# adaLN block with a spectral filter and an MLP, forward and backward: the last phase's operands, layouts and fillers rearranged

## The chip, the cores and the metric

The kernel runs on one core of a Trainium2 chip. The metric is the device time of one execution in microseconds (us). The kernel before took 500.65, 500.38 and 498.91 us in three runs: a median of 500.38. The profile is of one more execution, which took 503.03 us.

## The reference

The program computes a block and its gradients. Both come from this function and its vector-Jacobian product with `grad_out`.

```python
# x: (1, 2048, 512); c: (1, 512); w_mod: (512, 6*512); F = 1792
sa, ca, ga, sb, cb, gb = (silu(c) @ w_mod).reshape(1, 6, 1, 512) along axis 1
h = layernorm(x) * (1 + ca) + sa
x = x + ga * irfft2(rfft2(h) * (w_r + 1j * w_i))       # filter: 2048 x 257
h = layernorm(x) * (1 + cb) + sb
x = x + gb * (relu(h @ w1 + b1)**2 @ w2 + b2)
out_0 = x
out_1 .. out_9 = gradients of x, w_r, w_i, w1, b1, w2, b2, c, w_mod
```

All inputs and outputs are bf16.

## The kernel before

**Tiling.** The 2048 tokens are 16 tiles of 128 rows (NT = 16), in four blocks of 512 (NB = 4). F is 14 chunks of 128 (NFC = 14). The two-dimensional Fourier transform is a chain of matmuls with small DFT matrices. One dimension of 2048 is split as 16 x 128, so the spectrum is worked off in eight groups `gi`, each of which has a filter tile `Z[gi]` of 128 x 2 x 2 x 258 elements.

**Phases.** (1) Start-up: modulation rows, first layernorm, first DFT step (F1). (2) Spectral forward, `spec_f23`: for each group psB (L274) is evacuated to AE (L283, L285), psC (L261) uses AE and the DFT matrix LF, and `cmul` on DVE multiplies by Z. Matmuls of w2T and gT (L621, 224 of them, written to `gab`) serve as a filler here and in the next phase. `spec_g1` (L301, L314) uses a second matrix, LG. (3) `stage_g` and `stage_t` make the rows of the second layernorm from L332 and L346, block by block. (4) The MLP phase: `stage_h` (L771), `stage_o` (L794 with w2) and `stage_gn` (L794 with w1T), four blocks; `f1_again` and `late_f1` do the first DFT step of the backward pass there. (5) The last phase: the spectral backward `spec_f23` with filler `grad_w1` (L966, 256 matmuls) and `grad_b1` (L941, L953), then `spec_g1`, then for each pair of row tiles L332, L346 and the layernorm's backward rows, with filler `grad_w2` (L1037, 224 matmuls), `grad_b2` (L1048), and `GMod` (L413 to L425), which makes one of six column blocks of w_mod's gradient. The row sums acc1 (L1097) go over all 16 tiles, and the first two blocks of GMod need them.

**What sets the order.** Every engine runs its instructions in a fixed order, which is chosen when the program is built from the written order, priorities and a model of durations. All DMAs are issued by SyncE (SP), one after the other: an issue that waits for its data, or for its buffer, holds all DMAs written behind it. Eight DMA semaphores rotate, so a DMA also waits for the eighth DMA ahead of it to land. SBUF pools are stacked on the left and on the right; a tile that takes the place of an older one waits for the older one's last reader. So the place of a pool, too, decides when a load can start.

**The lines the change touches.** `load` (L989 to L992) reads, for one group of the last phase, a slice of LF (`LFb`), the filter in four to six pieces (`load_w`, L493) and the forward spectrum (`Xb`). Two groups are loaded ahead. `h2_sb` (h_sb in the profile, L998) is the operand of `grad_w1`, and `ghn_part` (L761) transposes the other operand, seven DMAs for each block. `load_hn` (L1032) transposes an operand of `grad_w2`, g_sb is the other. `n1` (L1080) and `gxl` are the rows that each pair needs. `w1T` (L666) is the transposed weight for `stage_gn`, w1 (L674) that of `stage_h`, `x1` (L693) the rows of x for `stage_g`.

Of the kernel before, what the change touches and what calls it, by code (L numbers as in the profile page):

```python
# [18 lines left out]
D = 512  # L19
# [142 lines left out]
def build_lf(tc, K, cpool, g):  # L162
# [32 lines left out]
    K["LF"] = LF  # L195
# [53 lines left out]
def spec_f23(tc, K, UT, AEs, dc, dest, elementwise, after=lambda gi: None):  # L249

    nc = tc.nc
    with tc.tile_pool(name="psB", bufs=1, space=PSUM) as psB_pool, \
         tc.tile_pool(name="psC", bufs=2, space=PSUM) as psC_pool:
        def f3(gi):
            ae = AEs[gi % 2]
            tl = dest(gi)
            for hh in range(2):
                ps = psC_pool.tile([P, 2, 512], FP32, name="psC")
                for o in range(2):
                    for cs in range(2):  # L260
                        nc.tensor.matmul(ps[:, o, 0:DF], lhsT=K["LF"][:, 2 * gi + hh, o + cs, :], rhs=ae[:, hh, 256 * cs:256 * cs + DF],  # L261
                                         start=(cs == 0), stop=(cs == 1))
                nc.scalar.copy(out=tl[:, hh, :, 0:DF], in_=ps[:, :, 0:DF])
# [137 lines left out]
class GMod:  # L401
# [3 lines left out]
    def __init__(self, tc, K, scf, gsc, wm_view, out9_view):  # L405
        self.__dict__.update(locals())

    def emit(self, jc, q, row, pool, ppool):
# [8 lines left out]
        for dc in range(0, 4, 2):  # L417
            wmc = pool.tile([P, 2, D], BF16, name="wmc", bufs=4)
            nc.sync.dma_start(wmc, self.wm_view[:, dc:dc + 2, cs])
            gwm = pool.tile([P, 2, D], BF16, name="gwm", bufs=4)  # L420
            for i in range(2):
                nc.scalar.activation(gwm[:, i, :], psb, AF.Copy, scale=self.scf[:, dc + i:dc + i + 1])
# [6 lines left out]
def kernel(  # L429
# [10 lines left out]
    gx1_dram = dram.tile([P, NT, D], BF16, name="gx1_dram")  # L440
    xs_dram = dram.tile([P, 8, 2, 2, FP], BF16, name="xs_dram")
# [71 lines left out]
    for b in range(NB):  # L513
# [94 lines left out]
    nc.sync.dma_start(LF_dram, K["LF"])  # L608
# [56 lines left out]
    w1T = wp.tile([P, NFC, D], BF16, name="w1T")  # L665
    nc.sync.dma_start(w1T, B_w1, transpose=True)  # L666
# [7 lines left out]
    nc.sync.dma_start(w1, w1_view)  # L674
    with tc.tile_pool(name="psR", bufs=1, space=PSUM) as psR, tc.tile_pool(name="psO", bufs=2, space=PSUM) as psO_pool, \
# [13 lines left out]
        def load_rows(b):  # L689
# [4 lines left out]
            if b > 0:  # L694
                gbt[b - 1] = rows.tile([P, TB, D], BF16, name="gb")
# [200 lines left out]
        for b in range(NB):  # L896
# [8 lines left out]
            else:  # L905
# [18 lines left out]
    K["LF"] = lf2.tile([P, 16, 3, P], BF16, name="LFb")  # L924
    lg2 = tc.alloc_tile_pool(name="lg2", bufs=1, side="right")
    K["LG"] = lg2.tile([P, 16, 3, P], BF16, name="LGb")
# [3 lines left out]
    h2_sb = gwa.tile([P, NT, D], BF16, name="h2_sb")  # L930
# [14 lines left out]
    def add_quadrants(ps, pool, out, scale=None):  # L945
# [5 lines left out]
        ps = mmps.tile([P, SB], FP32, name="mm")  # L951
        for i, x in enumerate((b4, b4l)):
            nc.tensor.matmul(ps[0:1, 0:w], lhsT=K["ones_col"], rhs=x, start=(i == 0), stop=(i == 1))  # L953
        row = pool.tile([1, w], BF16, name="b4r", bufs=2)
        nc.scalar.copy(out=row, in_=ps[0:1, 0:w])
        if scale is not None:
            nc.vector.tensor_tensor(row, row, scale, op=ALU.mult)
        nc.sync.dma_start(out, row)
# [16 lines left out]
    for fp in range(0, NFB, 2):  # L975
        for dc in range(4):
            for fb in (fp, fp + 1):
                units.append(lambda fb=fb, dc=dc: (grad_w1(fb, dc), dc == 3 and grad_b1(fb)))

    def fill_w1(n):  # L980
        for _ in range(n):
            if units:
                units.pop(0)()

    with tc.tile_pool(name="f23b", bufs=2) as fr, tc.tile_pool(name="ewb", bufs=2) as ew:
        Xt = {}

        def load(gi):
            nc.sync.dma_start(K["LF"][:, 2 * gi:2 * gi + 2], LF_dram[:, 2 * gi:2 * gi + 2])  # L989
# [8 lines left out]
        nc.sync.dma_start(h2_sb, h2_dram)  # L998
# [176 lines left out]
```

## Time and profile before

| what | value |
|---|---|
| median of three runs | 500.38 us |
| the profiled execution | 503.03 us, its span 501.3 us |
| mean granted TensorE clock | 0.968 |
| MLP phase, by the order of PE's lines | about 134 to 311 us |
| last phase: spectral backward | about 311 to 399 us |
| last phase: row tiles and grad_w2 | about 399 to 501 us |

The span is the time from the first to the last instruction. Times in the rows below are microseconds from its start unless marked ns. PE is TensorE's matmuls, PEld its weight loads, DVE VectorE, ACT ScalarE, SPq the DMA queue of SyncE. In an order row, `out<-in` names the tiles without buffer numbers, and the profile calls several tiles by short names: w is w1 or w2, h_dram may be h2_dram, n is n1, x is x1.

In the windows of 10 us, PE is busy 10.00 for most of 130 to 311, at a granted clock of 1.00. It has more gaps, and a clock under 1.00, in the last phase.

### The profile page before, as it was taken

Reading aid. Unit: us, or ns where it says so; the run is one execution under the profiler, and the core shown is the slowest. Engines: PE = TensorE matmul, PEld = TensorE weight load, DVE = VectorE, ACT = ScalarE, POOL = GpSimd, SP = SyncE. Lnnn points to the kernel's source line nnn. Section 1 sums busy time; section 2 is a strip of 40 time slices with the busy share of each in tenths; the row PEclk is TensorE's granted clock in tenths of the full one; section 3 lists DMA queues with packets and bytes.
Section 4 is the critical chain, followed back from the end, with each engine's and each line's share of the span. In section 5 each row is a group of like instructions: output and inputs, shape, how many; then the busy total and the mean of one; then the engine's idle time right before and its main releaser. Section 6 shows DMA issues by size and latency. Waiting matters only on the chain. (4 is left out here: it accounts for less than half of the span.)

```text
span 501.3 us, 7176 instructions
## 1 busy us (share of the span) xinstructions
PE 444.4 (89%) x2485; PEld 220.8 (44%) x2485; DVE 327.9 (65%) x747; ACT 264.8 (53%) x474; POOL 12.4 (2%) x56
## 2 busy tenths in 40 slices
PE   0848999999999999999979999699699899499993
PEld 0424466545444434434434444355255554144431
DVE  5878899588463577774958484174346464489946
ACT  3456766687461485466537563444242376267342
POOL 4121100000000000000000000000000000000000
PEclk9969999999999999999999999899799899799999
DMA  8964869931199499499349948756665399948995
GB/s 284 237 161 99 306 187 274 345 87 44 62 316 282 105 207 307 124 212 300 104 116 210 303 96 153 259 124 153 166 140 195 113 277 201 268 150 253 252 254 186
DMA packets 151708, 99.11 MB, mean 198 GB/s; under 512 B 99570, under 2 KB 137976, under 8 KB 151032
## 3 DMA queue, kind: packets, MB, share of 16 engines
q1 hardware_dynamic: 151672, 98.66, 73.5%
q8 instruction: 19, 0.31, 0.3%
q14 instruction: 17, 0.14, 0.1%
HBM read 35.43 MB, written 39.61 MB: 150 GB/s over the span
## 5 line engine op out<-in xcount | busy, mean ns | idle before, releaser
L621 PE MATMUL mm<-gT,w2T 128*128 128x512 bf16 x224 | 54.9, 378 | 2.3 <-ACT gab L626 1.1
L966 PE MATMUL mm<-gab,h_sb 128*128 128x448 bf16 x256 | 54.3, 370 | 1.2 <-DMA h_sb<-h_dram 1.2
L771 PE MATMUL mm<-h2T,w 128*128 128x512 bf16 x224 | 52.9, 379 | 2.6 <-DMA h2T<-h_dram 1.9
L1037 PE MATMUL mm<-g_sb,hn 128*128 128x512 bf16 x224 | 51.6, 382 | 1.8 <-DVE gw L1040 1.8
L794 PE MATMUL og<-w,h 128*128 128x512 bf16 x224 | 52.0, 379 | 0.0
L794 PE MATMUL og<-w1T,gab 128*128 128x512 bf16 x224 | 50.3, 379 | 0.0
L772 ACT ACTIVATE r<-mm,b1col 128x512 bf16<-128x512 f32 x56 | 37.9, 685 | 15.1 <-PE mm L771 10.2
L966 PEld LDWEIGHTS <-h_sb 128*128 128x128 bf16 x256 | 25.6, 102 | 26.0 <-issue 4.8
L771 PEld LDWEIGHTS <-w 128*128 128x128 bf16 x224 | 21.1, 97 | 32.2 <-issue 9.2
L1037 PEld LDWEIGHTS <-hn 128*128 128x128 bf16 x224 | 21.0, 98 | 30.2 <-issue 6.7
L794 PEld LDWEIGHTS <-gab 128*128 128x128 bf16 x224 | 21.9, 98 | 25.2 <-DVE gab L778 0.5
L621 PEld LDWEIGHTS <-w2T 128*128 128x128 bf16 x224 | 21.3, 97 | 25.6 <-issue 6.3
L794 PEld LDWEIGHTS <-h 128*128 128x128 bf16 x224 | 21.0, 98 | 24.9 <-issue 2.3
L774 DVE TENSOR_TENSOR h<-r 128x1024 bf16<-128x1024 bf16 x28 | 19.3, 691 | 16.8 <-ACT r L772 16.7
L624 DVE CAST gab<-mm 128x512 bf16<-128x512 f32 x28 | 19.2, 686 | 12.1 <-PE mm L621 11.7
L970 ACT CAST gw<-mm 128x448 bf16<-128x448 f32 x16 | 8.5, 533 | 31.5 <-PE mm L966 31.5
L423 DVE SCALAR_TENSOR_TENSOR gm_junk<-wmc,onef,gmbc 128x512 bf16<-128x512 bf16 x24 | 17.9, 748 | 8.2 <-DMA wmc<-in_w_mod_dram 7.1
L335 ACT ACTIVATE Tsb<-psT 128x512 bf16<-128x512 f32 x32 | 18.4, 599 | 7.9 <-PE psT L332 7.9
L379 DVE TENSOR_TENSOR p<-Z,G 128x1028 bf16<-128x1028 bf16 x8 | 5.6, 699 | 25.9 <-ACT AE L283 13.5
L626 ACT CAST gab<-mm 128x512 bf16<-128x512 f32 x28 | 16.4, 584 | 10.2 <-PE mm L621 10.0
L858 ACT CAST o<-og 128x512 bf16<-128x512 f32 x16 | 9.3, 581 | 20.9 <-PE og L794 20.9
L545 PE MATMUL mod_ps<-wm,scb 128*128 128x512 bf16 x24 | 9.6, 515 | 10.9 <-DVE scb L536 7.7
(265 smaller groups left out, 787.1 us busy)
## 6 DMA issues: line engine op xcount, KB each, us to landing
h_dram<-h SPq DMA_DIRECT2D x28, 256.0 KB, 3.5
gh_dram<-gab SPq DMA_DIRECT2D x28, 256.0 KB, 3.3
w<-in_B_w_dram SPq DMA_DIRECT2D x2, 1792.0 KB
wm<-in_w_mod_dram SPq DMA_DIRECT2D x3, 1024.0 KB, 9.4
wmc<-in_w_mod_dram SPq DMA_DIRECT2D x12, 256.0 KB, 3.8
out_dram<-gwm SPq DMA_DIRECT2D x12, 256.0 KB, 3.9
xs_dram<-Xs SPq DMA_DIRECT2D x8, 258.0 KB, 3.2
Xb<-xs_dram SPq DMA_DIRECT2D x8, 258.0 KB, 4.0
```

The costliest lines, as they stand in the source:

```text
L335: nc.scalar.activation(Tsb, ps, AF.Copy, scale=EF_S)
L423: nc.vector.scalar_tensor_tensor(out=junk, in0=wmc[:, i, :], scalar=K["onef"], in1=gmbc, op0=ALU.mult, op1=ALU.mult, accum_out=self.gsc[:, ...
L545: nc.tensor.matmul(ps, lhsT=scb[:, dc, :], rhs=wmt[j // 2][:, dc, (j % 2) * D:(j % 2 + 1) * D], start=(dc == 0), stop=(dc == 3))
L621: nc.tensor.matmul(ps, lhsT=w2T[:, dc, fc * P:(fc + 1) * P], rhs=gT[b][:, dc, :], start=(dc == 0), stop=(dc == 3))
L624: nc.vector.tensor_copy(out=gaT[b][:, fc, :], in_=ps)
L626: nc.scalar.copy(out=gaT[b][:, fc, :], in_=ps)
L771: nc.tensor.matmul(ps, lhsT=w1[:, dc, (fc + i) * P:(fc + i + 1) * P], rhs=h2T[b][:, dc, :], start=(dc == 0), stop=(dc == 3))
L772: nc.scalar.activation(r[:, i, :], ps, AF.Relu, bias=b1col[:, fc + i:fc + i + 1])
L774: nc.vector.tensor_tensor(h2, r, r, op=ALU.mult)
L794: nc.tensor.matmul(ps, lhsT=lhs(fc), rhs=rhs[:, fc, :], start=(fc == 0 and init is None), stop=(fc == NFC - 1))
L966: nc.tensor.matmul(ps[:, 0:W4], lhsT=h2_sb[:, t, dc * P:(dc + 1) * P], rhs=ghn[t // 4][:, t % 4, fs], start=(t == 0), stop=(t == NT - 1))
L1037: nc.tensor.matmul(ps, lhsT=hns[fc][:, t, :], rhs=g_sb[:, t, :], start=(t == 0), stop=(t == NT - 1))
```

## The change

1. In phase 1 each filter tile Z is also written to `wz_dram`, in the group's own layout (eight DMAs of 258 KB, after POOL has cleared the pad). In the last phase one DMA of 258 KB reads a group's Z.
2. LF for the last phase is in eight tiles. Four are loaded during the end of the MLP phase, four at the start of the last phase.
3. `w1T` moves to a pool of its own, which is released after the last `stage_gn`; its SBUF lies where LF and others were. `gb` moves to the pool of w2. `h2_sb` is loaded behind the last `stage_gn`, and the seven transposes of block 3 are merged into the last `stage_o`.
4. Four groups of Z and Xb are loaded ahead; LG is loaded one group earlier.
5. The second half of `grad_b1` and of `grad_b2` (the ones_col matmuls) is put off by one unit of filler; `grad_b1` is spread over other units.
6. Four of six `GMod` blocks are written into the spectral backward, at odd groups. The scaled rows `gwm` come from the bf16 copy in SBUF, half on ACT and half on DVE.
7. `n1` and `gxl` are loaded two pairs ahead; hn and g_sb are asked for ahead of `spec_g1`; the L332 step of the next pair is written ahead of its filler.
8. acc1 is summed in four quadrants of the array, even and odd rows apart, and the odd half is added at the end.

The core of the diff:

```diff
@@ phase 1
             for gi in range(8):
+                nc.gpsimd.memset(Z[gi][:, :, :, DF:FP], 0.0)
                 load_w(gi)
+                nc.sync.dma_start(wz_dram[:, gi], Z[gi])
@@ MLP phase, pools
-    w1T = wp.tile([P, NFC, D], BF16, name="w1T")
-    nc.sync.dma_start(w1T, B_w1, transpose=True)
...
     hring = tc.alloc_tile_pool(name="hring", bufs=7)
+    w1tp = tc.alloc_tile_pool(name="w1tp", bufs=1)
+    w1T = w1tp.tile([P, NFC, D], BF16, name="w1T")
+    nc.sync.dma_start(w1T, B_w1, transpose=True)
@@ MLP phase, end
+                K["LF"] = [cdp.tile([P, 2, 3, P], BF16, name=f"LFb{gi}") for gi in range(4)]
+                for gi in range(4):
+                    nc.sync.dma_start(K["LF"][gi], LF_dram[:, 2 * gi:2 * gi + 2])
                 merge(stage_gn(b, UT), [x for p in zip(again, parts + [lambda: None]) for x in p])
-                merge(stage_o(b), [lambda: None, lambda: None, late_f1.flush, lambda: None])
+                w1tp.release()
+                h2p = tc.alloc_tile_pool(name="h2p", bufs=1, side="right")
+                h2_sb = h2p.tile([P, NT, D], BF16, name="h2_sb")
+                nc.sync.dma_start(h2_sb, h2_dram)
+                parts = [lambda fc=fc: ghn_part(b, fc) for fc in range(0, NFC, 2)]
+                merge(stage_o(b), [x for p in zip([lambda: None] * 3 + [late_f1.flush] + [lambda: None] * 3, parts) for x in p])
@@ last phase, loads
-            nc.sync.dma_start(K["LF"][:, 2 * gi:2 * gi + 2], LF_dram[:, 2 * gi:2 * gi + 2])
-            load_w(gi)
-            Xt[gi] = fr.tile([P, 2, 2, FP], BF16, name="Xb")
+            if gi >= 4:
+                nc.sync.dma_start(K["LF"][gi], LF_dram[:, 2 * gi:2 * gi + 2])
+            nc.sync.dma_start(Z[gi], wz_dram[:, gi])
+            Xt[gi] = fr.tile([P, 2, 2, FP], BF16, name="Xb", bufs=4)
             nc.sync.dma_start(Xt[gi], xs_dram[:, gi])
-        for gi in range(2):
+        for gi in range(4):
             load(gi)
-        for fc in range(0, NFC, 2):
-            ghn_part(NB - 1, fc)
-        nc.sync.dma_start(h2_sb, h2_dram)
...
-            if gi + 2 < 8:
-                load(gi + 2)
-            if gi == 5:
+            if gi + 4 < 8:
+                load(gi + 4)
+            if gi == 4:
                 nc.sync.dma_start(K["LG"], LG_dram)
-            if gi > 0:
-                fill_w1(2)
+            fill_w1(2 if gi > 0 else 0)
+            if gi % 2 == 1:
+                gms.pop(0)()
@@ GMod
             for i in range(2):
-                nc.scalar.activation(gwm[:, i, :], psb, AF.Copy, scale=self.scf[:, dc + i:dc + i + 1])
+                if i == 0:
+                    nc.scalar.activation(gwm[:, i, :], gmbc, AF.Copy, scale=self.scf[:, dc + i:dc + i + 1])
+                else:
+                    nc.vector.tensor_scalar(gwm[:, i, :], gmbc, self.scf[:, dc + i:dc + i + 1], None, op0=ALU.mult)
@@ last phase, rows
+    load_rows3(0)
     load_hn()
     nc.sync.dma_start(g_sb, g_view)
+    load_rows3(2)
     for _ in range(3):
         load_hn()
+    CS = utcs.tile([P, NT, 4, 16, 8], BF16, name="utcs")
+    spec_g1(tc, K, Z, CS)
...
+        def colsums1(t, gh1, q1):
+            for q, row in ((0, gh1[:, 0, :]), (32, q1[:, 0, :]), (64, gh1[:, 1, :]), (96, q1[:, 1, :])):
+                nc.tensor.matmul(acc1[q:q + 32, :], lhsT=K["ones_q"], rhs=row, start=(t == 0), stop=(t == NT - 2), tile_position=(0, q))
...
+        Ts = g2_pair(0)
+        for t in range(0, NT, 2):
+            fill(1)
+            row_pair(t, Ts)
+            Ts = g2_pair(t + 2)
+            fill(1 if t % 4 == 0 and t < 12 else 0)
+            if t == 10:
+                grad_b2()
+        fill(1)
         late.flush()
-        acc1_sb = fp.tile([P, D], BF16, name="acc1_sb", bufs=1)
-        nc.vector.tensor_copy(acc1_sb[0:64, :], acc1[0:64, :])
+        acc1_odd = fp.tile([64, D], FP32, name="acc1_odd", bufs=1)
+        nc.scalar.copy(out=acc1_odd, in_=acc1[64:128, :])
+        acc1_sb = fp.tile([64, D], BF16, name="acc1_sb", bufs=1)
+        nc.vector.tensor_tensor(acc1_sb, acc1[0:64, :], acc1_odd, op=ALU.add)
```

The change also moves instructions on each engine. Three places follow, with the line numbers of the program they are from.

SP, between the spectral forward and `stage_g`, before: the last writes of the spectrum and of LG, then w1 (w_1473) and the rows of x.

```order
L635 DMA LG_dram<-LG 128x1536
L649 DMA xs_dram<-Xs 128x1032
L674 DMA w_1473<-in_B_w_dram 128x4x1792
L693 DMA x_1485<-in_A_x_dram 128x2048
L693 DMA x_1606<-in_A_x_dram 128x2048
L696 DMA gb<-in_grad_out_dram 128x2048 x2
```

The same place of SP in the changed program:

```order
L643 DMA LG_dram<-LG 128x1536
L657 DMA xs_dram<-Xs 128x1032
L680 DMA_TRANSPOSE w1T<-in_B_w_dram 128x14x512
L657 DMA xs_dram<-Xs 128x1032
L683 DMA w_1493<-in_B_w_dram 128x4x1792
L702 DMA x_1505<-in_A_x_dram 128x2048
L702 DMA x_1626<-in_A_x_dram 128x2048
```

The transpose of w1T, which stood eight rows later behind w2, now stands ahead of the last write of the spectrum, of w1 and of x.

SP, from the MLP phase's end into the last phase, before (gx_dram, rows of the gradient; out_dram<-x, rows of out_0; Z_3384, group 0's filter):

```order
L832 DMA gx_dram<-n2rows 128x1024
L761 DMA_TRANSPOSE gab<-gh_dram 128x4x256 x7
L832 DMA gx_dram<-n2rows 128x1024
L869 DMA out_dram<-x_2460 128x1024
L989 DMA LFb<-LF_dram 128x768 x2
L998 DMA h_sb<-h_dram 128x8192
L869 DMA out_dram<-x_2460 128x1024
L989 DMA LFb<-LF_dram 128x768 x3
L493 DMA Z_3384<-in_A_w_r_dram 64x2x257
```

The same stretch in the changed program:

```order
L922 DMA LFb_3097<-LF_dram 128x768
L889 DMA o<-gx_dram 128x1024 x2
L841 DMA gx_dram<-n2rows 128x1024
L927 DMA h_sb<-h_dram 128x8192
L770 DMA_TRANSPOSE gab<-gh_dram 128x4x256
L841 DMA gx_dram<-n2rows 128x1024
L770 DMA_TRANSPOSE gab<-gh_dram 128x4x256 x4
L878 DMA out_dram<-x_2480 128x1024
L770 DMA_TRANSPOSE gab<-gh_dram 128x4x256 x2
```

h_sb now stands ahead of the seven transposes, and four LFb loads (the last is shown) ahead of the two o loads.

PE, at the row sums of one pair of tiles in the last phase, before (gh and q are the rows that are summed):

```order
L1097 LDWEIGHTS ones_q
L1097 MATMUL acc_4296<-gh_4397,ones_q 32x512
L1097 LDWEIGHTS ones_q
L1097 MATMUL acc_4296<-q_4398,ones_q 32x512
L953 LDWEIGHTS ones_col
L953 MATMUL mm<-b_4483,ones_col 1x448
L1097 LDWEIGHTS ones_q
L1097 MATMUL acc_4296<-gh_4397,ones_q 32x512
L1097 LDWEIGHTS ones_q
L1097 MATMUL acc_4296<-q_4398,ones_q 32x512
```

A pair in the changed program:

```order
L1125 LDWEIGHTS ones_q
L1125 MATMUL acc_4450<-gh_5036,ones_q 32x512
L1125 LDWEIGHTS ones_q
L1125 MATMUL acc_4450<-q_5037,ones_q 32x512
L1125 LDWEIGHTS ones_q
L1125 MATMUL acc_4450<-gh_5036,ones_q 32x512
L1125 LDWEIGHTS ones_q
L1125 MATMUL acc_4450<-q_5037,ones_q 32x512
L1065 LDWEIGHTS hn
```

The four matmuls of a pair, each on a quadrant of its own, now stand together.

More of the change, by code (lines that the diff above doesn't have):

```diff
@@ L194, in build_lf @@
     LF = cpool.tile([P, 16, 3, P], BF16, name="LF")
-    K["LF"] = LF
+    K["LF"] = [LF[:, 2 * gi:2 * gi + 2] for gi in range(8)]
+    K["LFall"] = LF
     for q in range(4):
@@ L923 @@
     lf2 = tc.alloc_tile_pool(name="lf2", bufs=1, side="right")
-    K["LF"] = lf2.tile([P, 16, 3, P], BF16, name="LFb")
-    lg2 = tc.alloc_tile_pool(name="lg2", bufs=1, side="right")
-    K["LG"] = lg2.tile([P, 16, 3, P], BF16, name="LGb")
+    K["LF"] += [lf2.tile([P, 2, 3, P], BF16, name=f"LFb{gi}") for gi in range(4, 8)]
     W4 = 448
@@ L1094 @@
             nc.vector.tensor_tensor(q1, gh1, n1, op=ALU.mult)
+            late.add(lambda: colsums1(t, gh1, q1))
             for i in range(2):
-                late.add(lambda t=t + i, a=gh1[:, i, :], b=q1[:, i, :]: [
-                    nc.tensor.matmul(acc1[q:q + 32, :], lhsT=K["ones_q"], rhs=row, start=(t == 0), stop=(t == NT - 1), tile_position=(0, q))
-                    for row, q in ((a, 0), (b, 32))])
                 jk = fp.tile([P, D], BF16, name="jk1", bufs=1)
```

119 lines of the change are left out of this document (69 added, 50 removed).

## The prediction

> **What bounds the kernel now.** The profile page comes first, for the engine that sets the span.
>
> ```profile
> span 501.3 us, 7176 instructions
> PE 444.4 (89%) x2485; PEld 220.8 (44%) x2485; DVE 327.9 (65%) x747; ACT 264.8 (53%) x474; POOL 12.4 (2%) x56
> ```
>
> PE is busy for 89% of the span, and the change keeps all 2485 matmuls. So it can gain in three ways only: less PE idle time, fewer matmuls at a reduced clock, more matmuls side by side. The profiled execution took 503.03 us, 1.73 beyond its span and 2.65 above the median of the three runs (500.38). I sum against 503.03 and take 2.65 off at the end. The next view is what PE waited for from 305 us, where the last phase begins (columns: total, times, longest).
>
> ```profile
> PE acc L1097 <- DVE q L1094: 6.4, 1, 6.4
> PE psC L261 <- DMA LFb<-LF_dram: 4.3, 1, 4.3
> PE psB L274 <- ACT AE L283: 3.5, 3, 1.5
> PE mm L1132 <- DVE gcb L1130: 2.6, 1, 2.6
> PE psG L301 <- DVE utcs L306: 2.4, 1, 2.4
> PE mm L1037 <- DVE gw L1040: 1.8, 1, 1.8
> PE mm L966 <- DMA h_sb<-h_dram: 1.2, 1, 1.2
> PE mm L413 <- ACT gwm L422: 1.0, 2, 0.8
> PE mm L953 <- ACT b L949: 0.4, 1, 0.4
> ```
>
> These nine rows add up to 23.6 us, and each is a place that the change touches. The third view is the table by windows of 10 us (busy time and count of PE, PEld, DVE, ACT, POOL, then the granted clock, DMA share, GB/s).
>
> ```profile
> 320.00:330.00 10.00, 8.80 (x45) 4.71 (x45) 1.77 (x3) 3.78 (x7) 0.00 (x0) 0.83 0.54 165
> 340.00:350.00 10.00, 10.00 (x61) 5.85 (x60) 5.90 (x12) 4.36 (x9) 0.00 (x0) 1.00 0.63 138
> 390.00:400.00 10.00, 7.76 (x69) 5.13 (x69) 5.78 (x12) 3.37 (x6) 0.00 (x0) 0.83 0.32 107
> 430.00:440.00 10.00, 6.07 (x24) 2.06 (x24) 6.82 (x18) 2.25 (x4) 0.00 (x0) 0.66 0.90 283
> ```
>
> After each of the larger waits the granted clock falls, so a wait costs more than its idle time. An undisturbed window (340 to 350) has 1.00. The price shows in single rows of the timeline of PE:
>
> ```profile
> 357.99 4.29 PE L966 MATMUL mm<-gab,h_sb 128*128 128x448 bf16 x11
> 407.50 1.31 PE L966 MATMUL mm<-gab,h_sb 128*128 128x448 bf16 x6
> ```
>
> At full clock six of these take 1.31 with a drain of about 0.35, so 0.19 each; eleven would take 2.3 and took 4.29 after the wait at 356.99.
>
> **The change part by part: gains.**
>
> *Start of the last phase.* The operand h_sb is asked for late, on SP's queue (start, time):
>
> ```profile
> 295.36 10.01 SPq L761 DMA_TRANSPOSE gab<-gh_dram  x7
> 312.19 0.43 SPq L998 DMA_DIRECT2D h_sb<-h_dram  x1
> ```
>
> It is issued at 312.19, behind ten microseconds of transposes, so L966, the filler that could cover the three AE waits, cannot run before 322. The change issues it ahead of the transposes, when the last w1T matmul ends (about 295). Then L966 stands ready at 311 and covers 3.5 + 1.2 = 4.7 of idle time, and the 0.83 clock of 320:330 (0.17 x 10 = 1.7) goes. What is late next is the first evacuation in the phase, about 0.9 that nothing hides. Gain 5.5; the bounds are 2 (the AE waits stay) and 6.4.
>
> *LF and Z.* The 4.3 wait for LFb has its cause in these rows of SP's own waits:
>
> ```profile
> SPq L1006 <- DVE gW L382: 8.0, 2, 5.1
> SPq L493 <- DMA out_dram<-x: 6.3, 1, 6.3
> SPq L989 <- PE og L794: 4.0, 1, 4.0
> ```
>
> SP issues in order; an L1006 output that waits for DVE holds the LFb and Z loads behind it. With four groups in hand, and one Z load in place of four to six, a load has three to four groups (8 us of PE each) to spare. Gain 4.3 of waiting and 2.6 of clock (2.0 on the eleven matmuls above, 0.6 on their neighbours): 6.9. The eight writes and reads of Z cost SP about 0.4 each beside PE work; I count nothing, since SP idles between the loads there, and 0.4 x 8 = 3 if it did not.
>
> *G1.* The 2.4 wait for utcs comes from DVE standing behind gc work that waited for output DMAs. In the new order the gc work stands behind all the utcs evacuations, so it can hold none of them; the DMAs go out as before. I take 2.4 plus 0.17 x 10 = 1.7 of clock, less 0.3: 3.8 (bounds 0 and 4.1).
>
> *n1.* The 6.4 wait is q for an n load issued behind three hn transposes; now n1 is fetched two pairs ahead. Gain 6.4 + 0.4 (the b wait, deferred) + clock: the 430:440 window at 0.66, of which PE worked 6.07, loses about 2.2. Together 9.0.
>
> *End.* The 1.8, the 1.0 and the 2.6 rows: four of six modulation blocks leave the end, so DVE is free for gw, and L1037 fills between the last two. Of 5.4, I leave 1.0 for the gcb chain: 4.4. The blocks themselves move to the spectral phase, where DVE is 5.90 of 10 busy (340:350).
>
> ```profile
> L423 DVE SCALAR_TENSOR_TENSOR gm_junk<-wmc,onef,gmbc 128x512 bf16<-128x512 bf16 x24 | 17.9, 748 | 8.2 <-DMA wmc<-in_w_mod_dram 7.1
> ```
>
> A block has four of these (3.0) and, new on DVE, two scalings of the same shape; each is bounded by nothing and by the 0.75 of this row. That is 3.0 to 4.5 per block, one block in two groups (16 us): DVE goes from 5.9 to about 8.5 of 10. Hidden, but the cover is thin: each DVE wait that shows costs its length, counted under new waits.
>
> *Row sums.* The matmuls on acc stand like this now, in two quadrants, and, in the MLP phase, four at once:
>
> ```profile
> 438.83 0.39 PE L1097 MATMUL acc<-q,ones_q 128*32 128x512 bf16 x1
> 438.83 0.39 PE L1097 MATMUL acc<-gh,ones_q 128*32 128x512 bf16 x1
> 439.06 0.38 PE L1097 MATMUL acc<-q,ones_q 128*32 128x512 bf16 x1
> 439.37 2.98 PE L1037 MATMUL mm<-g_sb,hn 128*128 128x512 bf16 x13
> 443.15 0.39 PE L1097 MATMUL acc<-gh,ones_q 128*32 128x512 bf16 x1
> ...
> 311.22 0.39 PE L682 MATMUL acc<-gp,ones_q 128*32 128x512 bf16 x1
> ...
> 311.45 0.38 PE L682 MATMUL acc<-gp,ones_q 128*32 128x512 bf16 x1
> ```
>
> Four matmuls of one pair hold PE for 0.23 + 0.31 + 0.38 = 0.92 (the fourth alone, at 443.15). Four at once, as L682, hold it for 0.23, and 0.31 up to a full-array matmul. Eight pairs save 8 x 0.6 = 4.9; one add at the end and an evacuation of acc1's odd half cost about 0.9 that L1037 only partly hides. Gain 3.8 (3 to 5).
>
> Gains: 5.5 + 6.9 + 3.8 + 9.0 + 4.4 + 3.8 = 33.4.
>
> **Costs.**
>
> *Early phase.* w1T is placed where LF was, and its load moves from 135 us to a place ahead of the last xs_dram write, w1 and x:
>
> ```profile
> 79.87 1.06 PE L261 MATMUL psC<-AE,LF 128*128 128x257 bf16 x8
> 87.83 0.37 SPq L649 DMA_DIRECT2D xs_dram<-Xs  x1
> 88.30 0.42 SPq L674 DMA_DIRECT2D w<-in_B_w_dram  x1
> 90.62 0.28 PE L314 MATMUL psF<-LG,Z 128*1 128x128 bf16 x8
> 98.77 0.69 DVE L717 TENSOR_TENSOR yg<-y,modb 128x1024 bf16<-128x1024 bf16 x1 [0.51 <-DMA x<-in_A_x_dram]
> 135.10 11.62 SPq L666 DMA_TRANSPOSE w1T<-in_B_w_dram  x1
> 124.66 9.97 PE L621 MATMUL mm<-gT,w2T 128*128 128x512 bf16 x44 [0.26 <-ACT gab L626]
> ```
>
> w1T may go when the last L261 has read LF, 10.0 us before G1 ends (80.9 to 90.9). Its issue took 11.62 at 135, behind the 1.8 MB of w2; half of that, about 6, is the lower end. So it ends 4.0 before to 1.6 after G1's end. w1 follows at -3.5 to +2.1; now w1 goes out at 2.6 before G1's end, and x is there 10 us after w1 (88.30 to 98.26), when DVE has already waited 0.51. So x comes 0.9 earlier to 4.7 later. The row of xs_dram has the same spread, and ACT's first Tsb waits for that write. Behind the waiting DVE L717 stand the evacuations L624 of the filler, and PE behind them, so a wait passes on nearly whole. From issue near 8.5, between the ends, 1.8 of waiting. Also 57 of the L621 fillers (0.227 each, 12.9 us) move ahead of G1: no more work, but the tail at 124.66, in which DVE and ACT could catch up, goes; 1.2 for that, 1 for the clock. Cost 4.0, bounds -1 and 9.
>
> In sentences that the sum does not need: the Trainium skill, "DMA: Bandwidth & Descriptors", section "Latency and other measured facts", gives a DMA transpose 261 GB/s, by which the 1.8 MB of w1T take an estimated 7.0 us. By that x would wait 0.3 in place of 1.8.
>
> *End of the MLP phase.* Four LFb loads of 0.4 stand ahead of the loads that DVE L881 waits for:
>
> ```profile
> 283.72 3.60 SPq L880 DMA_DIRECT2D o<-gx_dram  x2
> 287.98 0.69 DVE L881 TENSOR_TENSOR o<-o,modb 128x1024 bf16<-128x1024 bf16 x1 [5.30 <-DMA o<-gx_dram]
> ```
>
> 1.6 later, of which PE's order leaves about 0.6 of slack: cost 1.0 (0 to 2).
>
> *New waits in the last phase.* g_sb, hn, n1 and the blocks' loads now come together around G1, so something is late that was not. The nearest rows are the waits that go, so one is bounded by 0 and 6.4. I take one of 2 us and 1 of clock: 3.0.
>
> Costs 8.0; net 25.4. 503.03 - 25.4 = 477.6, less 2.65: **475**.
>
> On the clock: the window 390:400 shows 0.83 after a wait of only 2.4. The Trainium skill, "TensorE: Matmul & The Clock Gate", "HAM oscillation — how this bites in real kernels", has the clock fall for PE gaps over about 3.4 us. By the trace a new wait of 2 us carries clock loss; by the page it carries none, the 2 us of it above go, and the time is 473. The row speaks against the page here.
>
> **The rivals.**
>
> 1. *The early phase costs nothing* (w1T's issue takes 6, x comes in time) and no new wait shows: 475 - 4 - 3 = 468. For it: DVE waits only 0.51 for x now, and lower bounds are met. Against: the row of 11.62.
> 2. *DVE and DMA become the limit* in stage_g and the last phase: early cost 9, new waits of 6.4 with clock 2.2: 475 + 5 + 5.6 = 486. For it: DVE near 8.5 of 10 and the loads crowded at G1. Against: PE has long filler there.
> 3. *The start wait stays* (the change doesn't do what it says): h_sb and seven transposes share the DMA, and the first L966 still waits. Price: the 5.5 of that term: 480.
> 4. *Slower than before.* SP's order holds Z or Xb in every group of the spectral phase: each load stands behind outputs that wait for DVE, as L1006 did for 8.0. Eight waits of 2 are 16; a clock as in 430:440 (0.66) over the phase's 88 us (311 to 399) loses 30: 475 + 46 = 521. It decides once a group's wait is over about 1 us. Against: four groups' lead, some 30 us.
>
> **How the numbers follow.** Forecast 0.60, rivals 0.13, 0.12, 0.10 and 0.05. The forecast with its bounds spans 466 to 484; rival 1 at 468 and 3 at 480 lie in it. The range goes to 464 below (rival 1 with fuller gains) and 488 above (rival 2), so that about 0.15 is left out. 0.5% is 2.5 us, about what a measurement of this kernel can tell from no change. Faster 0.95; of rival 4's 0.05, where only half of the groups wait the time comes out near no change: same 0.02, slower 0.03.
>
> **What would show it.** Right: the waits of L1097, L261 and L301 gone, L966 within 3 us of the last L794, acc in groups of four, granted clock 1.00 from 311 on. Wrong: DVE's L717 waiting over 5 for x or ACT for xs_dram; PE idle ahead of L1037 for g_sb or hn; DVE's p waiting for Z in several groups; PE waiting for L881 over 2.

## The result, and the profile after

The changed kernel took 475.89 us (median of 4 runs, 475.21 to 476.55) against 500.51 for the kernel before in the same comparison: a ratio of 0.9512, with a 95% interval of 0.9483 to 0.9542. Its profiled execution took 475.21 us, 27.8 less than that of before (503.03); the prediction had 477.6 for it and 475 for the median.

First the head of the profile page of the changed kernel, then what PE waited for from 312 us to the end (total, times, longest).

```profile
span 473.4 us, 7172 instructions
PE 432.9 (91%) x2485; PEld 218.3 (46%) x2485; DVE 331.2 (70%) x759; ACT 257.0 (54%) x463; POOL 12.7 (3%) x64
```

```profile
PE psC L262 <- ACT G L264: 3.1, 1, 3.1
PE psB L275 <- ACT AE L284: 0.5, 2, 0.4
PE psG L302 <- ACT utcs L309: 0.2, 1, 0.2
```

The nine rows of before (23.6 us) have become three (3.8 us). One of them is new. The windows say the same of the clock (columns as in the prediction):

```profile
320.00:330.00 10.00, 6.79 (x35) 3.65 (x34) 2.66 (x6) 4.68 (x9) 0.00 (x0) 0.83 0.72 221
430.00:440.00 10.00, 10.00 (x70) 4.94 (x67) 9.47 (x19) 4.59 (x11) 0.00 (x0) 1.00 1.07 279
```

Of the windows from 310 to 470, only the one with the new wait is under 1.00; the window 430 to 440, at 0.66 before, is full. To see where the time went, the program is cut at five places that both kernels have. These are PE's timeline rows of the changed kernel at these places: the last forward psF, the first matmul with w1T, the last with w2, the last backward psF, the last of grad_w2.

```profile
104.43 0.28 PE L315 MATMUL psF<-LG,Z 128*1 128x128 bf16 x8
163.14 12.25 PE L803 MATMUL og<-w1T,gab 128*128 128x512 bf16 x56
311.56 3.20 PE L803 MATMUL og<-w,h 128*128 128x512 bf16 x14
391.99 0.33 PE L315 MATMUL psF<-LGb,Z 128*1 128x128 bf16 x10
462.83 7.08 PE L1065 MATMUL mm<-g_sb,hn 128*128 128x512 bf16 x32
```

And the same places of the kernel before (the first of them stands in the prediction, at 90.62):

```profile
160.20 12.25 PE L794 MATMUL og<-w1T,gab 128*128 128x512 bf16 x56
308.10 3.19 PE L794 MATMUL og<-w,h 128*128 128x512 bf16 x14
398.90 0.28 PE L314 MATMUL psF<-LGb,Z 128*1 128x128 bf16 x8
491.51 3.61 PE L1037 MATMUL mm<-g_sb,hn 128*128 128x512 bf16 x16 [1.84 <-DVE gw L1040]
```

Start plus time, or the start alone for the first w1T matmul, give the cuts and the stretches between them:

| stretch | before | after | difference | predicted |
|---|---|---|---|---|
| start to first w1T matmul ("early") | 160.20 | 163.14 | +2.9 | +4.0 |
| to the last w2 matmul ("MLP") | 151.09 | 151.62 | +0.5 | +1.0 |
| to the last backward psF ("spectral") | 87.89 | 77.56 | -10.3 | -13.2 |
| to the end of grad_w2 ("row part") | 95.94 | 77.59 | -18.4 | -15.6 |
| tail | 6.18 | 3.49 | -2.7 | -1.6 |

In the predicted column, spectral is the sum of the start, LF and Z, and G1 less the new waits, the row part has n1, the row sums and 2.8 of the end, and the tail has the rest of the end. The last psF is the end of G1 in the kernel before, where no psG matmul follows it. In the changed kernel 24 of the 64 psG matmuls still follow:

```profile
392.45 2.78 PE L302 MATMUL psG<-LGb,Z 128*128 128x256 bf16 x24
```

They end at 395.23. With the cut there, the spectral stretch takes 80.5 (7.4 less than before) and the row part 74.7 (21.3 less). Some other work moved from the row part into the spectral stretch: four L413 (L415 in the changed kernel) of about 0.3, and two `grad_b1` of 0.94 with their ones_col matmuls, some 4 us. With all of it counted where it was, the spectral stretch gained about 11.4 (13.2 predicted), and the row part and the tail together about 20.0 (17.2 predicted).

### The profile page after: what moved, and what is told of

Read it like the earlier page. It is cut to its first block, busy times and chain, and to the rows that moved or that the text cites. A ratio compares the mean times of both kernels' runs of the same rounds, so it can differ in the third digit from the quotient of the medians.

```text
span 473.4 us, 7172 instructions
## 1 busy us (share of the span) xinstructions
PE 432.9 (91%) x2485; PEld 218.3 (46%) x2485; DVE 331.2 (70%) x759; ACT 257.0 (54%) x463; POOL 12.7 (3%) x64
## 4 chain that ended last, share of the span: by engine, by line
PE 65%; DVE 11%; DMA 8%; ACT 6%; SPq 5%; issue 2%; POOL 1%; DVEq 0%; ACTq 0%
PE og L803 13%; PE mm L1065 10%; PE mm L780 10%; PE mm L993 10%; PE mm L629 3%; PE psG L302 3%; PE psC L262 2%; PE psT L333 2%; PE psY L347 2%; SPq L770 2%; PE psB L275 2%; DMA o<-gx_dram 2%; DVE l_st L569 2%; DMA n_dram<-x_sb 1%; DMA x<-in_A_x_dram 1%
## 5 line engine op out<-in xcount | busy, mean ns | idle before, releaser
L993 PE MATMUL mm<-gab,h_sb 128*128 128x448 bf16 x256 | 52.8, 360 | 0.0
L1065 PE MATMUL mm<-g_sb,hn 128*128 128x512 bf16 x224 | 50.2, 380 | 0.0
L993 PEld LDWEIGHTS <-h_sb 128*128 128x128 bf16 x256 | 25.4, 99 | 22.0 <-issue 1.8
L816 ACT CAST G<-og 128x512 bf16<-128x512 f32 x16 | 9.3, 580 | 19.0 <-PE og L803 19.0
L347 PE MATMUL psY<-Tsb,TAT 128*128 128x256 bf16 x128 | 18.1, 272 | 1.5 <-ACT Tsb L336 1.4
```

Source lines behind the costliest of these rows:

```text
L347: nc.tensor.matmul(psY[:, H * s:H * s + H], lhsT=K["TAT"][:, s * e], rhs=Tsb[:, H * e:H * e + H], start=(e == 0), stop=(e == 1))
L993: nc.tensor.matmul(ps[:, 0:W4], lhsT=h2_sb[:, t, dc * P:(dc + 1) * P], rhs=ghn[t // 4][:, t % 4, fs], start=(t == 0), stop=(t == NT - 1))
L1065: nc.tensor.matmul(ps, lhsT=hns[fc][:, t, :], rhs=g_sb[:, t, :], start=(t == 0), stop=(t == NT - 1))
```

## The experiments

Every experiment is the changed kernel with one edit, unless it says otherwise. The table gives the stretches of each run's profiled execution, worked out from the same five places, and the median time with that of the kernel before measured beside it. Runs with the same number in the last column were measured on one chip (496.20, 498.08 and 497.04 are of three chips).

| run | forward G1 ends | G1 to first w1T | MLP | spectral | row part | tail | median us | before |
|---|---|---|---|---|---|---|---|---|
| after | 104.7 | 58.4 | 151.6 | 77.6 | 77.6 | 3.5 | 475.89 | 500.51 |
| after_again | 104.2 | 58.4 | 151.7 | 77.5 | 77.6 | 3.5 | 475.39 | 497.04 |
| w1t_behind | 107.2 | 55.1 | 153.7 | 77.1 | 77.4 | 4.1 | 472.78 | 496.20 |
| h2_late | 104.2 | 57.6 | 154.3 | 75.1 | 77.4 | 3.7 | 474.32 | 496.20 |
| h2_place | 107.7 | 58.3 | 151.2 | 78.9 | 77.6 | 3.6 | 478.83 | 497.04 |
| two_ahead | 105.1 | 58.5 | 151.3 | 75.2 | 77.4 | 3.7 | 474.42 | 496.20 |
| z_pieces | 106.7 | 58.2 | 152.0 | 84.7 | 77.4 | 3.7 | 484.36 | 496.20 |
| acc_two | 104.6 | 58.2 | 154.8 | 75.5 | 79.0 | 3.7 | 475.62 | 498.08 |
| no_prefetch | 104.3 | 57.9 | 154.0 | 74.3 | 83.6 | 3.8 | 479.32 | 498.08 |
| gm_end | 107.3 | 58.1 | 151.6 | 78.7 | 74.6 | 20.2 | 490.85 | 498.08 |
| gm_mid | 104.7 | 57.9 | 152.3 | 77.8 | 91.4 | 3.5 | 490.44 | 497.04 |
| g_low | 107.5 | 57.1 | 152.5 | 76.6 | 78.0 | 3.7 | 476.50 | 498.08 |
| best | 106.9 | 55.6 | 151.5 | 73.7 | 77.6 | 3.7 | 469.89 | 497.04 |

The first column and the MLP column vary by over 3 us in code that the edits leave alone, so a median cannot show an effect of one or two. The stretch that an edit touches can, where it is steady in the runs that leave it alone. G1 to the first w1T matmul is (57.1 to 58.5), and so is the row part (77.4 to 78.0). The spectral stretch is not: it takes 74.3 to 77.6 in five runs with the same spectral code (after, after_again, w1t_behind, acc_two, no_prefetch), so it shows no effect under about 3.

The 24 psG matmuls behind the last psF, 2.9 us to their end, stand in the row part of every run but gm_end and gm_mid, where G1 is done at the cut. Beside these two, the changed kernel's stretches are 80.5 and 74.7.

### The early stretch: w1t_behind

```diff
-    nc.sync.dma_start(w1T, B_w1, transpose=True)
...
         load_rows(0)
+        nc.gpsimd.tensor_copy(w1T[:, 0, 0:1], x1b[0][:, 0, 0:1])
+        nc.sync.dma_start(w1T, B_w1, transpose=True)
         merge(stage_g(0))
```

> The changed kernel, but the transposed load of w1T is held back until the first rows of x are in (a one-element copy of x1 on POOL writes into w1T first). Changed kernel: 475.9 us median; first w1T matmul at 163.1 us, 2.9 later than before. Theory: that loss comes from SP, where w1T's issue of 8.8 us stands ahead of the last xs_dram write and of w1 and x; then ACT's first Tsb (PE wait 1.4) and DVE's L727 (wait 2.0 for x) no longer wait, the first w1T matmul comes at 160.3 to 161.5 and the time is 473 to 474.5. Rival: the loss comes from the fillers that moved ahead (no tail of L629 any more); then the first w1T matmul stays within 0.5 of 163.1 and the time within 0.7 of 475.9.

In the changed kernel, SP's and DVE's timelines and PE's row read like this:

```profile
98.67 8.82 SPq L680 DMA_TRANSPOSE w1T<-in_B_w_dram  x1
107.59 0.52 SPq L657 DMA_DIRECT2D xs_dram<-Xs  x1
```

```profile
117.26 0.69 DVE L727 TENSOR_TENSOR x<-yg,x 128x1024 bf16<-128x1024 bf16 x1 [2.04 <-DMA x<-in_A_x_dram]
```

```profile
111.45 0.60 PE L347 MATMUL psY<-Tsb,TAT 128*128 128x256 bf16 x4 [1.41 <-ACT Tsb L336]
```

The issue of 8.82 held the xs_dram write to 107.59, 2.9 after G1's end; in the kernel before that write went out 3.1 ahead of it. With the transposes behind x, SP's and DVE's rows are:

```profile
101.65 0.70 SPq L657 DMA_DIRECT2D xs_dram<-Xs  x1
111.35 0.81 SPq L701 DMA_DIRECT2D x<-in_A_x_dram  x2
116.31 6.79 SPq L902 DMA_TRANSPOSE w1T<-in_B_w_dram  x1
```

```profile
115.54 0.69 DVE L725 TENSOR_TENSOR yg<-y,modb 128x1024 bf16<-128x1024 bf16 x1 [0.51 <-DMA x<-in_A_x_dram]
```

DVE waits 0.51 for x, as before the change, PE's wait for Tsb is gone, and G1 to the first w1T matmul takes 55.1 in place of 57.1 to 58.5 in the runs without this edit. The absolute time of 160.3 to 161.5 was missed (162.3), since the forward G1 ended 2.5 later in this execution; the stretch from there is what the edit changes. The median of 472.78 lies in the theory's range to within 0.3, but h2_late and two_ahead, measured beside it without this edit, took 474.32 and 474.42, so the medians show only about 1.6. The stretch shows that the loss came from SP's order, as the theory had it.

### The start of the last phase: h2_late, h2_place and g_low

```diff
 # h2_late
                 h2_sb = h2p.tile([P, NT, D], BF16, name="h2_sb")
-                nc.sync.dma_start(h2_sb, h2_dram)
...
+    nc.sync.dma_start(h2_sb, h2_dram)
     W4 = 448
 # h2_place
-                h2p = tc.alloc_tile_pool(name="h2p", bufs=1, side="right")
...
     gwa = tc.alloc_tile_pool(name="gwa", bufs=1)
+    h2_sb = gwa.tile([P, NT, D], BF16, name="h2_sb")
+    nc.sync.dma_start(h2_sb, h2_dram)
```

> The changed kernel, but h2_sb (h_sb in the profile) is asked for at the start of the last phase, behind the seven transposes, as before the change. Theory (the term of 5.5): L993 cannot start before about 322, the AE waits come back with a wait for h_sb and a clock under 1.00; 480 to 482. Rival: the wait of 3.1 for ACT's G and its clock loss are there in the changed kernel anyway and lie at the same place, so that only 2 to 3 are lost: 478 to 479.

> The changed kernel with h2_sb (h_sb) back in the place it had before the change, the pool that stands where w2 was, so that its load must wait for the last L803 matmul; everything else as changed. Theory (the place, not the place in SP's order, made the late start): h_sb is issued after the MLP phase's end (314 to 319) and lands 6 to 10 later; L993 starts at 323 or later, PE waits 4 or more, the stretch from the MLP phase's end to G1's end takes 80 to 83 (75 to 77.6 in the runs so far): 479 to 482. Rival (the wait for G hides it as in h2_late): the stretch stays under 78 and the time under 477.

Neither forecast of the theory held. With h2_late the load goes out at 309.66 (298.82 in the changed kernel), PE waits 1.7 for h_sb and 0.9 for G, and the spectral stretch takes 75.1, not more than the 74.3 to 77.6 of runs that keep the load early; the time is under both ranges. With h2_place the mechanism of the theory came: the load goes out at 322.20 and L993 (L992 there) starts only at 332.3. Yet the stretch takes 78.9, just 1.4 more than in the changed kernel, which is within its spread. The median lies 3.4 above that of after_again, but 3.5 of what the profiled execution lost lies ahead of the end of the forward G1, in code that the edit leaves alone. Its waits from 312 us show why the stretch grows so little:

```profile
PE psB L275 <- ACT AE L284: 4.6, 5, 1.5
PE psG L302 <- ACT utcs L309: 0.2, 1, 0.2
```

The AE waits come back (4.6), but the wait of 3.1 for G, which lies at the same place in the changed kernel, is absent. The change took one wait away and put another in its place. What that other one is shows in the changed kernel's SP and PE rows, with what SP waited for ahead of the first Z load:

```profile
318.73 0.41 SPq L878 DMA_DIRECT2D out_dram<-x  x1
319.19 0.43 SPq L1024 DMA_DIRECT2D LFb<-LF_dram  x1
324.39 0.33 SPq L1025 DMA_DIRECT2D Z<-wz_dram  x1
```

```profile
SPq L1025 <- DMA out_dram<-x: 4.7, 1, 4.7
```

```profile
325.22 1.28 PE L262 MATMUL psC<-AE,LFb 128*128 128x257 bf16 x8 [3.05 <-ACT G L264]
```

The last write of out_0 goes out at 318.73, behind two transposes, three LFb loads and two wmc loads, and lands at about 324. Its rows were ready at 317.6, so the queue held it for 1.1 at most; the rest is the write itself. G and Z lie in SBUF that the MLP phase's rows held, so both wait for it. For G the profile of the changed kernel names a wmc load, but in gm_mid and gm_end, where no wmc load stands there, it names out_dram<-x, and in these runs and the changed kernel G starts within 0.1 us of the first Z load's issue. g_low takes G out of that region, and puts the early modulation blocks' tiles into it.

```diff
-        spec_f23(..., lambda gi: fr.tile([P, 2, 2, FP], BF16, name="G"), ew_b, after_b)
+        spec_f23(..., lambda gi: gwa.tile([P, 2, 2, FP], BF16, name="G", bufs=2), ew_b, after_b)
...
-    gms = [lambda j=j, q=q, row=row: gm.emit(j, q, row, gwa, mmps)
+    gms = [lambda j=j, q=q, row=row: gm.emit(j, q, row, fr, mmps)
```

> The changed kernel with G in the pool that stands where w2 was, and the four early GMod blocks' tiles in the pool that stands where x1 was, so that ACT's first G no longer waits for the last write of out_0 (issued 318.7, G at 324.5). Theory: PE's wait of 3.1 at psC L262 and the clock loss of 1.7 in 320 to 330 go: 471 to 472.5. Rival: DVE's first cmul still waits for Z0 and Xb until 327, so the wait moves to the next G and the time stays within 1 of 475.9.

The wait for G is gone, but DVE still begins with Z at 327.6 and a later wait appears, as the rival had it. The first row is of DVE, the second of PE's waits:

```profile
327.61 0.70 DVE L380 TENSOR_TENSOR p<-Z,G 128x1028 bf16<-128x1028 bf16 x1 [7.07 <-ACT gw L997]
```

```profile
PE mm L972 <- DVE b4l L967: 2.1, 1, 2.1
```

The releaser named for DVE is not the last one: ACT had been done, and Z0 was issued only at 324.7, behind out_0. The spectral stretch took 76.6.

### LF and Z: two_ahead and z_pieces

```diff
 # two_ahead
-        for gi in range(4):
+        for gi in range(2):
             load(gi)
...
-            if gi + 4 < 8:
-                load(gi + 4)
+            if gi + 2 < 8:
+                load(gi + 2)
 # z_pieces
-            nc.sync.dma_start(Z[gi], wz_dram[:, gi])
+            load_w(gi)
```

> The changed kernel with two groups of Z, Xb and LF loaded ahead in place of four, Z still in one DMA a group. Theory (the lead is what removed the wait for LFb): PE waits for LFb or DVE for Z in at least one group, 2 to 4 us each with clock loss: 479 to 483. Rival (the one DMA a group is what removed it): within 1 of 475.9.

> The changed kernel with four groups ahead, but the filter read again from the inputs in four to six DMAs a group. Theory (the lead suffices): 475.5 to 477. Rival (SP's queue and the short rows were the cause): DVE waits for Z, PE for G, 479 or more.

Two groups ahead cost nothing that the stretch can show (75.2). The filter in pieces costs 7 to 10 (84.7 against 74.3 to 77.6), though four groups are ahead. So in the changed kernel the one DMA a group is what pays, and the lead is not. The wait in z_pieces is not the LFb one of the kernel before, however. PE's wait, ACT's row behind it, and SP's row of the load that DVE's gm_junk needs:

```profile
PE mm L993 <- ACT gmbc L417: 6.2, 1, 6.2
```

```profile
376.78 0.59 ACT L417 CAST gmbc<-mm 128x512 bf16<-128x512 f32 x1 [7.16 <-DVE gm_junk L428]
```

```profile
368.26 0.42 SPq L421 DMA_DIRECT2D wmc<-in_w_mod_dram  x1
```

SP spends 2.5 us a group on the pieces, and the load of wmc, which stands behind them and behind outputs, comes late; ACT's next block waits for DVE, and the evacuations of L993 wait behind ACT.

### The row part: acc_two, no_prefetch

```diff
 # acc_two
-            for q, row in ((0, gh1[:, 0, :]), (32, q1[:, 0, :]), (64, gh1[:, 1, :]), (96, q1[:, 1, :])):
+            for q, row in ((0, gh1[:, 0, :]), (32, q1[:, 0, :])):
...
+            for q, row in ((0, gh1[:, 1, :]), (32, q1[:, 1, :])):
...
-        nc.vector.tensor_tensor(acc1_sb, acc1[0:64, :], acc1_odd, op=ALU.add)
+        nc.vector.tensor_copy(acc1_sb, acc1[0:64, :])
 # no_prefetch
-            load_rows3(t + 4)
...
+            load_rows3(t)
             n1, gxl = rows3[t]
```

> The changed kernel with acc1 summed in two quadrants again (the four matmuls of a pair still stand together; the add of the odd half at the end is left out). Theory A (the quadrants make the gain of 3.8): one more slot of 0.23 in each of eight pairs, 1.8 in all, less the add: 477 to 478, so that the other 2 of the 3.8 come from standing together. Rival: PE is not the limit there and nothing shows: within 0.5 of 475.9.

> The changed kernel with n1 and gxl of each pair loaded only when the pair is worked on, as before the change. Theory (the term of 9.0): the wait for q behind an n1 load comes back, 4 to 7 with clock loss of about 2: 481 to 485. Rival: with hn and g_sb asked for earlier the n1 loads no longer stand behind the transposes, so only 0 to 3 are lost: 476 to 479.

Two quadrants cost 1.4 in the row part (79.0 against 77.6), near the 1.8 of the theory; the median (475.62) does not resolve it. The rest of the 3.8 would then come from the four matmuls standing together, which was not run by itself. Without the prefetch the row part takes 83.6, 6.0 more, in two waits (1.8 for q and 1.0 for gw) and a clock of 0.70 in the window from 420. PE's wait, and SP's and DVE's rows behind it:

```profile
PE acc L1123 <- DVE q L1142: 1.8, 1, 1.8
```

```profile
410.89 7.12 SPq L1060 DMA_TRANSPOSE hn<-h_dram  x3
418.68 0.43 SPq L1085 DMA_DIRECT2D n<-n_dram  x1
```

```profile
422.79 0.69 DVE L1142 TENSOR_TENSOR q<-gh,n 128x1024 bf16<-128x1024 bf16 x1 [7.89 <-DMA n<-n_dram]
```

So the mechanism is the one of the prediction, an n load behind three hn transposes, against the rival. But PE's work covers most of the 7.9, so the wait is 1.8 in place of 4 to 7, and the median, 479.32, lies between the ranges of theory and rival. The 6.0 are two thirds of the term of 9.0.

### The modulation blocks: gm_end and gm_mid

```diff
 # both
             fill_w1(2 if gi > 0 else 0)
-            if gi % 2 == 1:
-                gms.pop(0)()
...
-    gms = [lambda j=j, q=q, row=row: gm.emit(j, q, row, gwa, mmps)
+    gms = [lambda j=j, q=q, row=row: gm.emit(j, q, row, endp["gm"], psX)
 # gm_end
-        while units2:
+        while units2 or gms:
             fill(1)
+            if gms:
+                gms.pop(0)()
 # gm_mid
                 units2.pop(0)()
                 run_later()
+                if gms and len(units2) % 2:
+                    gms.pop(0)()
```

> The changed kernel with the four GMod blocks back at the end, after the two that need acc1. Theory (the term of 4.4): DVE is late with gw and gcb again, PE waits 4 to 6 ahead of L1065 and at the last transpose: 479 to 481. Rival: DVE, freed in the spectral phase, gives 1 to 2 back there: 477 to 479.

> The changed kernel with the four GMod blocks between units of grad_w2, beside the row tiles, in place of the spectral backward. Theory (their price at the end was DVE's, 3.8 a block, and DVE has 8 to 9.5 of 10 busy in 430 to 470): 15 us of DVE work do not fit, PE waits for gw, q or acc_sb; the stretch from G1's end to the last L1065 (77.4) grows by 4 to 8, the one before shrinks by 0 to 2: 478 to 482. Rival (only blocks after the filler's end cost, as in gm_end): 474 to 477.

Both cost far more than any theory had: 15 each. At the very end (gm_end) PE waits for the blocks alone. Two of PE's waits, and the windows of the tail (busy times, clock, DMA share, GB/s):

```profile
PE mm L415 <- ACT gmbc L417: 8.1, 3, 3.8
PE mm L1189 <- DVE gcb L1187: 7.5, 1, 7.5
```

```profile
470.40:488.00 17.60, 1.93 (x5) 0.30 (x5) 14.61 (x43) 7.68 (x12) 0.00 (x0) 0.63 0.63 202
```

With no filler left, a block takes about 4.2 from one L415 to the next, of which DVE works 3.4. The tail grows by 16.7, the row part does not grow (74.6 against 74.7), and the spectral stretch is 1.8 shorter (78.7 against 80.5), of the size that the rival had, but within that stretch's spread. The DMA share of 0.63 says that this cost is the chain of the blocks, above all DVE's work, and not traffic.

In gm_mid there is filler, and still the row part takes 91.4 in place of 74.7, again 16.7 more, while the spectral stretch is 2.7 shorter. DVE's waits in that stretch:

```profile
DVE gm_junk L428 <- DMA wmc<-in_w_mod_dram: 7.5, 2, 7.3
DVE gn L1140 <- ACT gh L1139: 5.5, 2, 3.9
DVE q L1143 <- DMA n<-n_dram: 3.6, 1, 3.6
```

The windows of the whole row part, cut at the end of G1, first of gm_mid, then of the changed kernel, then of the kernel before:

```profile
392.70:484.10 91.40, 82.63 (x445) 39.52 (x441) 68.80 (x173) 43.10 (x90) 0.00 (x0) 0.94 0.96 254
```

```profile
395.20:469.90 74.70, 74.55 (x437) 37.69 (x434) 57.96 (x133) 36.88 (x78) 0.00 (x0) 1.00 1.00 254
```

```profile
399.20:495.00 95.80, 86.14 (x476) 39.47 (x476) 64.72 (x152) 51.11 (x104) 0.00 (x0) 0.96 0.90 233
```

DVE is at 69 of 91 in gm_mid, but the DMA share is 0.96. A block reads and writes 0.5 MB each, so four of them are 4.2 MB. At 254 GB/s gm_mid moves 23.2 MB in its row part and the changed kernel 19.0 in its own: the blocks' bytes at the same rate, 16.5 us, are the whole difference. In the spectral stretch the changed kernel's share is 0.72.

That the rate is a bound is argued, not shown. A share of 1 is no strict ceiling, since single windows show 1.07 and more, and the row part of gm_end moved 266 GB/s in the same 74.7 us; at that rate an estimate for gm_mid's 23.2 MB is 87 us, 12.5 of the 16.7. A rival is the order of the loads. The first wmc load stands behind three hn transposes, and DVE, which takes its work in order, waits for it while gw and q stand behind:

```profile
411.88 8.13 SPq L1058 DMA_TRANSPOSE hn<-h_dram  x3
420.68 0.43 SPq L421 DMA_DIRECT2D wmc<-in_w_mod_dram  x1
```

```profile
423.62 0.75 DVE L428 SCALAR_TENSOR_TENSOR gm_junk<-wmc,onef,gmbc 128x512 bf16<-128x512 bf16 x1 [7.29 <-DMA wmc<-in_w_mod_dram]
```

No run loads wmc ahead of these transposes, so how much of the cost is bytes and how much is order stays open. Either way it is the DMAs and not DVE's work that is late in gm_mid.

### The changed kernel again, and a better one: after_again and best

```diff
+    ewp = tc.alloc_tile_pool(name="ewp", bufs=2, side="right")   # p of cmul
+    spa = tc.alloc_tile_pool(name="spa", bufs=1)                  # Z and X of groups 0 and 1
...
-                for gi in range(4):
-                    nc.sync.dma_start(K["LF"][gi], LF_dram[:, 2 * gi:2 * gi + 2])
...
+                parts.insert(5, lambda: [nc.sync.dma_start(K["LF"][gi], LF_dram[:, 2 * gi:2 * gi + 2]) for gi in range(4)])
```

with the edits of w1t_behind and g_low.

> The changed kernel itself once more, for its time on the chip of the next runs: 475.9 if chips agree; runs so far differ by 3 to 6 us on another chip, and identical code differs by up to 3 us in its first 105 us.

> The changed kernel with three mends: w1T's load behind x (as in w1t_behind), the first four LFb loads behind h2_sb and five transposes (so that the o loads come first), and Z, X and G of the first two groups and the products p in SBUF that held neither x1 nor its neighbours, so that nothing in the first two groups waits for out_0. Theory: the early stretch loses 2.9 less, the wait for o L890 (1.9) goes to about 0.3, the wait at the last phase's start (3.1, or 2.1 for b4l as in g_low) goes, with its clock: 6 to 8 us under after_again. Rival: only the early 2.9 shows, since DVE or DMA is late for something else in the first groups: 2 to 4 under after_again.

best took 469.89 (468.33 to 473.6, 6 runs) against 475.39 (471.65 to 479.02) for the changed kernel measured beside it: 5.5 less by the medians. Its ratio to the kernel before is 0.9461 (0.9419 to 0.9503), that of after_again 0.955 (0.95 to 0.9601); by these ratios the gain is 4.4, and the intervals just touch. By stretches it gains 2.8 early, and the wait for o is gone, though a longer one for h2T leaves the MLP stretch as it was. The spectral part takes 73.7: 3.8 less than after_again, but only 0.6 less than the lowest of the five runs with unchanged spectral code, so the size of that gain is not shown. The time lies between theory and rival. In its spectral stretch DVE begins at 321.2, six earlier than in g_low, and of PE's waits for DVE there is left:

```profile
321.19 0.70 DVE L380 TENSOR_TENSOR p<-Z,G 128x1028 bf16<-128x1028 bf16 x1 [3.76 <-ACT G L264]
```

```profile
PE mm L976 <- DVE b4l L971: 1.0, 1, 1.0
```

## Why the prediction was right

The number came out (475 against 475.89), but in part by luck: some terms were wrong and made up for each other.

- *Early phase* (+4.0): +2.9, by the cause named, though two of its readings were off. w1T went out 6.0 before G1's end, not 10.0, since SP's writes at 97.77 and 98.18 stand ahead of it; its issue took 8.82 where 8.5 was assumed. So x came 4.7 later against G1's end than before, the upper end of the range, but DVE was later too, and its wait of 2.0 is near the 1.8 assumed by chance. w1t_behind takes 2.0 to 3.4 less than the runs without it. The 261 GB/s of the Trainium skill ("DMA: Bandwidth & Descriptors", "Latency and other measured facts") would make an estimated 7.0 of the issue; it took 6.8 when it went out behind x, and 8.8 among the other DMAs. (In the row of before, x is there at 98.77, when the wait of 0.51 ends; 98.26 is its start.)
- *End of the MLP phase* (+1.0): PE's wait for o rose from 0.3 to 1.9. The four LFb loads held SP for 2.23 (from 285.55), not 1.6; that would fit a slack of 0.6, which no run measures. Other waits there fell, so the stretch lost 0.5.
- *Start of the last phase* (-5.5): the waits went as said, but a wait of 3.1, and 1.7 of clock, came at the same place. Undoing the load's place adds only 1.4 to the stretch, within its spread.
- *New waits* (+3.0): one came, of 3.1 with 1.7 of clock, 4.8 in all. Its place was not foreseen: G and Z waiting for out_0, not g_sb, hn or n1.
- *LF and Z* (-6.9): z_pieces costs 7 to 10, but by another wait than the LFb one of the term, so that the size agrees is luck. The step "a load has three to four groups to spare" was not what did it: two_ahead loses nothing that shows. Rival 4 was right that SP can hold the loads of each group, but in z_pieces by the issues themselves and not by outputs that wait for DVE (0.2 of SP's waits from 318 to 372, against 9.4 in the changed kernel, where no load comes late by them).
- *G1* (-3.8): the wait fell from 2.4 to 0.2 and the clock there is 1.00. It was not undone by itself.
- *n1* (-9.0) and *row sums* (-3.8): undoing them costs 6.0 and 1.4. Both terms were sized with the clock loss and with lone matmuls of the kernel before.
- *End* (-4.4): this is the step that failed. "DVE is free for gw" took the blocks for work of DVE, and sized them by the 5.4 of three waits. Undoing this part costs 15. At the end of the program that is indeed DVE's chain, 4.2 a block; among the filler it is their DMAs, in a stretch whose share was 0.90 before. By an estimate, 0.90 of 95.8 us, done in the 74.7 of the changed kernel's row part, would be a share of 1.15. The windows of before had the share (0.90 of DMA at 430 to 440 is quoted in the prediction); it was not used. In the spectral stretch DVE then had 6.7 of 10 busy (51.56 of 77.5), not 8.5: the scalings take 0.35 each, and the 5.9 was one window of a stretch with a mean of 4.6.

The sum of the last three, 17.2, is 2.8 under the 20.0 that the row part and the tail gained: n1 and row sums were taken too large and the end far too small. The spectral sum of 13.2 is 1.8 over its 11.4, and the two costs ahead of it together 1.6 over theirs. So the profiled execution gained 27.8 where 25.4 were forecast, and the medians differ by 24.6, since the profiled execution of before was a long one. What each undone part costs does not add up to the gain either, so the parts are not independent; a likely reason is that with the blocks back DMA is late anyway, so that prefetch or quadrants could not show.

On the clock: at one place, the wait for G, waits of 3.05 and 2.5 (after, w1t_behind) were followed by a window at 0.83 and 0.86, waits of 2.7 and 2.3 (acc_two, two_ahead) by none, while in no_prefetch waits of 1.8 and 1.0 lie in a window at 0.70. So neither side of the prediction's comparison holds: a gap under the 3.4 us of the Trainium skill ("TensorE: Matmul & The Clock Gate", "HAM oscillation — how this bites in real kernels") can cost clock, and one of 2.7 need not.

## What to carry to other kernels

Read the DMA share of the stretch beside the waits: where it is near 1, as in the row part here, moving traffic to a stretch with room can be worth more than the engine's waits show (15 us here for waits of 5.4). When a load is taken ahead, look at what it now stands in front of on the same queue, here a transpose of 8.8 us before a small write that everything waited for. And when a wait at a phase's start goes, look for the next one at that place, above all for reused SBUF whose last reader is an output DMA.

## What was not expected of the hardware

The first part, up to the end of the forward G1, is the same code in most runs and took 104.2 to 107.7. The longer ones (106.7 and up) had a wait at the modulation matmuls (mod_ps) of 2.2 to 3.4 and a window from 40 at a clock of 0.84, where the others had 1.2 to 1.8 and 1.00. In the MLP phase, the window from 260 had 0.72 to 1.00 and that from 290 had 0.83 or 1.00, after waits for h2T, v and o that differ by little over 1 in runs with the same code there. So nearly the same waits came with 0 to 3 us of loss, and single executions of this kernel differ by that much; what decides it is not shown.
